# SyncE's transfers chained in the order of the plan, in an attention and feed-forward kernel of 394 tiles

## The chip, the cores and the metric

The kernel runs on one core of one Trainium2 chip. A core has five engines that each work through their own list of instructions in order: TensorE (PE in the profile, its weight loads PEld), VectorE (DVE), ScalarE (ACT), GpSimd (POOL) and SyncE (SP). In this kernel SP does no arithmetic: it issues all the transfers between DRAM and the core's memory, and within it, one after the other, and where a transfer must wait for something, SP waits with it. The transfers themselves are done by 16 DMA engines. The metric is the device time of one execution in microseconds (us), as the median of several runs.

## The reference, cut to what matters

Four batches of 12608 tokens with 128 channels attend to the keys through 49 agents, and the result goes through a feed-forward block of width 1024 with SoLU and a normalization.

```python
a2k = softmax(scale * agents @ k.T);  agent_v = a2k @ v      # per batch
q2a = softmax(scale * q @ agents.T);  x = q2a @ agent_v      # 50432 tokens in all
h = x @ w_in                                                 # 128 -> 1024
solu = h * softmax(h)
ln = (solu - mean(solu)) / sqrt(var(solu) + 1e-6) * g_ln
out = ln @ w_out                                             # 1024 -> 128
```

## The kernel before

The tokens of all four batches are laid end to end and cut into 394 tiles of 128, so that a tile can lie across two batches. Three kinds of work run interleaved.

*Per batch* (`phase_a`): the keys come in 13 blocks (tile kt, `kload`, L647), the values likewise (vt, `vload`, L658). PE multiplies the agents with a block of keys (L669), DVE and ACT make the running softmax, PE multiplies with the values (L723). In the end one matrix per batch is left, split in a high and a low part (mh, ml), which already holds w_in. The buffer kt is single (from the second batch on): a block can be loaded only when PE is through with the block before it. The same holds for vt.

*Per eight tiles* (`phase_b`): a load of queries (qt, `qload`, L891, also one buffer), PE's logits against the agents (L911), their softmax, and a transposed copy pT.

*Per tile*: PE makes ph = pT x (mh, ml) (L1027), DVE its maximum (nm, L1032), ACT the exponential (L1042), DVE the product u (L1047), ACT the square sum (L1053). Then 1024 x 128 of u must be transposed and multiplied with w_out, and units of four tiles alternate between two ways. A Y unit is transposed in blocks by DVE (tb, L1067) and moved into place by 16 transfers (uY, L1077), and PE multiplies it in one pass (L1083); its output oy (L1091 or L1093) is scaled by yp. A Z unit is transposed by PE (L1060), copied by ACT (uT), split by POOL (uH, uL) and multiplied by PE in three passes (L1154); DVE scales the product in place of a tile rB (L1238).

The scale factors yp and rB come by a detour: POOL computes them for two units, DVE turns them (yr, L1195), one transfer stores them in DRAM (dr, `send`, L1199), and two more read them back in the shapes that are wanted (yp, `senty`, L1225; rB, `sent`, L1204, spread over all partitions). L1238 frees a PSUM bank that PE needs for its next products, and the result goes out from the same tile (L1244).

What sets the order: every piece of work is an `op` of a planner (`Plan`) with its engine, an estimated cost, and a rank from a table. `plan.run` plays all engines through in modelled time, picks at each step the ready piece with the lowest rank, and writes its instructions down at that moment. This gives one list for all engines in the order of the plan. Afterwards the framework's own scheduler goes over the list and orders the instructions of each engine anew by its own estimates, unless a dependency holds them. The last lines of the kernel put such dependencies in, each instruction on the one before it on its engine, without a semaphore ("NoSync"), but for the engines in `engs` only:

```python
for ins in list(nc.cur_bb.bb.instructions)[marks:]:
    if ins.engine not in engs:
        continue
    if ins.engine in prev:
        tc.add_manual_dep(ins, prev[ins.engine], nosync, reason="order")
    prev[ins.engine] = ins.name
```

Before, `engs` (L451) holds PE, ACT, DVE and POOL; SP's transfers are left to the framework's scheduler.

Of the kernel before, what the change touches and what calls it, by code (L numbers as in the profile page):

```python
# [335 lines left out]
def kernel(  # L336
# [111 lines left out]
    DFX = 8.0  # L448
    ASTART = 4.99
    AEND = -155.17  # L450
    engs = (mybir.EngineType.PE, mybir.EngineType.Activation, mybir.EngineType.DVE, mybir.EngineType.Pool)  # L451
    SCALE = 1.0 / math.sqrt(C)
    INV = 1.0 / DF
    LIFT = DF ** 1.5
# [1098 lines left out]
```

## Time and profile before

| | us |
|---|---|
| median of 3 runs | 1466.27 (1463.65 to 1466.43) |
| profiled execution, its own time | 1469.04 |
| span in the profile, first to last instruction | 1467.3 |
| busy: PE, DVE | 1429.0, 1369.8 |
| busy: ACT, POOL | 1273.6, 978.4 |
| mean granted clock of PE, share of full speed | 0.992 |

Busy time is the union of an engine's instructions. Issuing transfers is not counted as busy, so SP has no row; its issues show in the timeline as SPq. A row of a timeline gives start, duration, engine, line, operation, tiles, and in brackets the idle time before and what ended it. Where rows are merged, x tells how many instructions they hold.

### The profile page before, as it was taken

To read this page: it belongs to the slowest core of one execution; us is meant where nothing else is said; L and a number is where in the kernel's file an instruction comes from. 1 tells how busy PE (TensorE), PEld (TensorE's weight loads), DVE (VectorE), ACT (ScalarE), POOL (GpSimd) and SP (SyncE) were. 2 spreads that over 40 slices of the span, in tenths; PEclk is the share of its full clock that TensorE was granted. 3 is DMA by queue.
4 is the path that set the end of the run, shared out by engine and by line. 5 is a ranking of instruction groups with operands and counts; after the bars stand their busy time and mean duration, and the time that the engine had idled before them with its cause. 6 is when DMAs were issued, how large, how long until landed. Compare 5 with 4: busy or idle time off the path is not lost.

```text
span 1467.3 us, 32448 instructions
## 1 busy us (share of the span) xinstructions
PE 1429.0 (97%) x11965; PEld 1268.3 (86%) x11965; DVE 1369.8 (93%) x1979; ACT 1273.6 (87%) x2424; POOL 978.4 (67%) x1125
## 2 busy tenths in 40 slices
PE   8799999999999999999999999989999999999998
PEld 4678899898898889989998888878988899999888
DVE  7899999999999989999999999979997999999985
ACT  5599999989889879989989899978987899889985
POOL 3476668766766766775766767666675678677664
PEclk9899999999999999999999999999999999999999
DMA  9456664564555475556546755545644555455351
GB/s 365 149 158 181 176 192 131 142 158 109 148 160 175 136 200 137 169 166 173 147 105 163 182 165 154 159 131 138 156 110 122 141 141 138 124 131 133 92 125 63
DMA packets 111647, 221.71 MB, mean 151 GB/s; under 512 B 46208, under 2 KB 49152, under 8 KB 111488
## 3 DMA queue, kind: packets, MB, share of 16 engines
q1 hardware_dynamic: 111488, 219.63, 54.7%
q8 instruction: 95, 1.56, 0.5%
q14 instruction: 64, 0.52, 0.1%
HBM read 92.87 MB, written 26.02 MB: 81 GB/s over the span
## 4 chain that ended last, share of the span: by engine, by line
PE 65%; DVE 16%; DMA 7%; ACT 6%; issue 3%; SPq 3%; POOL 1%; DVEq 0%; ACTq 0%
PE ph L1027 18%; PE px L1083 16%; PE px L1154 13%; PE px L1060 8%; DVE u L1047 5%; DVE nm L1032 5%; DMA rB<-dr 3%; ACT e L1042 3%; PE px L723 3%; DVE tb L1067 3%; PE px L911 2%; SPq L1077 2%; PE px L669 2%; ACT e L1053 2%; PE px L956 1%
## 5 line engine op out<-in xcount | busy, mean ns | idle before, releaser
L1042 ACT ACTIVATE e<-ph,nm 128x1024 f32<-128x1024 f32 x394 | 441.2, 1123 | 82.4 <-DVE nm L1032 79.3
L1047 DVE SCALAR_TENSOR_TENSOR u<-ph,e 128x1024 f32<-128x1024 f32 x394 | 471.6, 1216 | 26.4 <-ACT e L1042 23.4
L1053 ACT ACTIVATE e<-u,su 128x1024 bf16<-128x1024 f32 x394 | 455.1, 1160 | 33.1 <-DVE u L1047 32.7
L1032 DVE TENSOR_REDUCE nm<-ph 128x1 f32<-128x1024 f32 x394 | 464.9, 1205 | 13.5 <-PE ph L1027 12.8
L1138 POOL TENSOR_TENSOR uL<-uT,uH 128x1024 fp32r<-128x1024 f32 (+1 forms) x197 | 468.4, 2379 | 11.7
L1134 POOL TENSOR_SCALAR uH<-uT 128x1024 fp32r<-128x1024 f32 (+1 forms) x197 | 206.6, 1049 | 278.9 <-ACT uT L1125 273.3
L1083 PE MATMUL px<-w,uY 128*128 128x128 f32 x3072 | 374.4, 276 | 0.1
L1083 PEld LDWEIGHTS px<-w,uY 128*128 128x128 f32 x3072 | 357.8, 192 | 5.4 <-issue 2.3
L1027 PE MATMUL ph<-mh,pT 128*128 128x512 f32 x784 | 332.8, 424 | 7.0 <-DVE u L1047 6.9
L1027 PE MATMUL ph<-ml,pT 128*128 128x512 f32 x784 | 311.0, 397 | 0.0
L1067 DVE STREAM_TRANSPOSE tb<-u 128x1024 f32<-128x1024 f32 x192 | 235.4, 1233 | 0.8
L1154 PE MATMUL px<-uH,wH 128*128 128x256 f32 x808 | 233.2, 289 | 2.4 <-DVE rB L1238 1.3
L1125 ACT COPY uT<-px 128x512 f32<-128x512 f32 x392 | 220.1, 591 | 15.3 <-PE px L1060 13.8
L1060 PE MATMUL px<-ident,u 128*128 128x128 f32 x1616 | 226.4, 275 | 6.9 <-DVE u L1047 2.9
L1154 PE MATMUL px<-uL,wH 128*128 128x256 f32 x808 | 225.2, 279 | 0.0
L1154 PE MATMUL px<-uH,wL 128*128 128x256 f32 x808 | 225.2, 279 | 0.0
L1060 PEld LDWEIGHTS px<-ident,u 128*128 128x128 f32 x1616 | 186.4, 141 | 34.1 <-DVE u L1047 3.2
L1027 PEld LDWEIGHTS ph<-mh,pT 128*128 128x128 f32 x784 | 149.0, 190 | 47.0 <-DVE u L1047 19.9
L1027 PEld LDWEIGHTS ph<-ml,pT 128*128 128x128 f32 x784 | 149.6, 191 | 21.6
L1154 PEld LDWEIGHTS px<-uH,wH 128*128 128x128 f32 x808 | 152.4, 189 | 6.9 <-issue 2.7
L1154 PEld LDWEIGHTS px<-uL,wH 128*128 128x128 f32 x808 | 152.9, 189 | 2.3 <-issue 0.5
L1154 PEld LDWEIGHTS px<-uH,wL 128*128 128x128 f32 x808 | 152.3, 188 | 0.0
(134 smaller groups left out, 1465.4 us busy)
## 6 DMA issues: line engine op xcount, KB each, us to landing
uY<-tb SPq DMA_DIRECT2D x768, 128.0 KB, 2.4
qt<-in_qT_dram SPq DMA_DIRECT2D x49, 512.0 KB, 4.6
kt<-in_kT_dram SPq DMA_DIRECT2D x36, 512.0 KB, 4.9
vt<-in_v_dram SPq DMA_DIRECT2D x36, 512.0 KB, 4.5
rB<-dr SPq DMA_DIRECT2D x50, 256.0 KB, 4.1
out_dram<-rB SPq DMA_DIRECT2D x50, 256.0 KB, 2.4
out_dram<-oy SPq DMA_DIRECT2D x48, 256.0 KB, 2.5
kh<-in_kT_dram SPq DMA_DIRECT2D x12, 512.0 KB, 10.2
```

What stands on the lines that cost most here:

```text
L1027: nc.tensor.matmul(phs[x][:, sl], lhs, mats["mh" if m == 0 else "ml"][:, sl], start=(m == 0 and h != 1), stop=(m == 1 and h != 0))
L1032: nc.vector.tensor_reduce(out=nms[x], in_=phs[x], op=ALU.max, axis=AX.X, negate=True)
L1042: nc.scalar.activation(out=es[x], in_=phs[x], func=AF.Exp, bias=nms.pop(x), accum_out=st[G]["S"][:, j : j + 1])
L1047: nc.vector.scalar_tensor_tensor(out=u, in0=phs[x], scalar=INV, in1=es[x], op0=ALU.mult, op1=ALU.mult, accum_out=su)
L1053: nc.scalar.activation(out=sq, in_=u, func=AF.Square, bias=su, scale=-float(DF), accum_out=st[G]["Q"][:, j : j + 1])
L1060: nc.tensor.transpose(pt[:, kf * P : (kf + 1) * P], us[x][0][:, k0 * P : (k0 + 1) * P], ident)
L1067: nc.vector.transpose(to, us[x][0].rearrange("p (k r c) -> p k r c", r=GT, c=SQB))
L1083: nc.tensor.matmul(st[G]["po"][:, a * P : (a + 1) * P], yb[G][1][:, a, kf].rearrange("p x c -> p (x c)"), w2[:, kf, :], start=(kf == 0), s ...
L1125: nc.scalar.copy(out=rr[x][:, hf * 4 : hf * 4 + 4, :], in_=pt)
L1134: nc.gpsimd.tensor_scalar(out=uH, in0=rr[x][:, k0:k1, :], scalar1=1.0, scalar2=0.0, op0=ALU.mult, op1=ALU.add)
L1138: nc.gpsimd.tensor_tensor(out=uL, in0=rr[x][:, k0:k1, :], in1=uH.bitcast(F32), op=ALU.subtract)
L1154: nc.tensor.matmul(po, wt[:, kf, :], ut[:, kf, :], start=(q == 0), stop=(q == WM - 1))
```

## The change

SP is added to the engines whose instructions are chained.

```diff
-    engs = (mybir.EngineType.PE, mybir.EngineType.Activation, mybir.EngineType.DVE, mybir.EngineType.Pool)
+    engs = (mybir.EngineType.PE, mybir.EngineType.Activation, mybir.EngineType.DVE, mybir.EngineType.Pool, mybir.EngineType.SP)
```

The lists of PE, DVE, ACT and POOL stay as they are. Of SP's 1182 transfers 15 change places against the others: the first loads of keys and values of three batches, one further block of keys, two loads of queries near them, two outputs of Y units, and two pairs of yp and rB. The first keys of the third batch go 113 places back, its first values 43; the first keys and values of the fourth 22 each; the two outputs 18 and 19; the others 2 or 3 places forward or back. In the rows below a name ends in a running number of the program.

SP in the last batch, the transfers around the eleventh block of its keys (kt_10), before:

```order
L1199 DMA dr_12059<-yr_12057 16x2x32
L647 DMA kt_10_12188<-in_kT_dram 128x1024
L1225 DMA yp_12106<-dr_12059 128x4x1
L1204 DMA rB_12110<-dr_12059 128x512
L1244 DMA out_dram<-rB_12110 128x512
L891 DMA qt_12199<-in_qT_dram 128x1024
```

The same place with the change:

```order
L1199 DMA dr_12059<-yr_12057 16x2x32
L1225 DMA yp_12106<-dr_12059 128x4x1
L1204 DMA rB_12110<-dr_12059 128x512
L1244 DMA out_dram<-rB_12110 128x512
L647 DMA kt_10_12188<-in_kT_dram 128x1024
L891 DMA qt_12199<-in_qT_dram 128x1024
```

The keys have moved from in front of yp and rB to behind the output of rB.

SP after the last batch's keys, at two pairs of yp and rB some 30 us apart (a piece of the difference, - before, + with the change):

```order
 L1199 DMA dr_13823<-yr_13821 16x2x32
-L1077 DMA uY_13883<-tb_13506 32x1024 x2
 L1225 DMA yp_13844<-dr_13823 128x4x1
 L1204 DMA rB_13848<-dr_13823 128x512
-L1077 DMA uY_13883<-tb_13506 32x1024 x14
+L1077 DMA uY_13883<-tb_13506 32x1024 x16
 L1244 DMA out_dram<-rB_13848 128x512
```

Two pieces of uY that stood ahead of yp and rB now stand behind them; at the second pair it reads the same.

SP at the start of the third batch, where its first keys and values (kt_0, vt_0) now stand, with the change:

```order
L891 DMA qt_5026<-in_qT_dram 128x1024
L1244 DMA out_dram<-rB_4898 128x512
L647 DMA kt_0_5115<-in_kT_dram 128x1024
L658 DMA vt_0_5121<-in_v_dram 128x1024
L891 DMA qt_5170<-in_qT_dram 128x1024
L1244 DMA out_dram<-oy_5165 128x512
L1077 DMA uY_5177<-tb_4966 32x1024 x9
```

Before, kt_0 stood more than a hundred transfers earlier, and the queries qt_5170 behind the first two pieces of uY.

## Rows read from the trace of the kernel before

**Rows 1.** The page, part 1: busy us, share of the span, instructions of each engine.
```profile
PE 1429.0 (97%) x11965; PEld 1268.3 (86%) x11965; DVE 1369.8 (93%) x1979; ACT 1273.6 (87%) x2424; POOL 978.4 (67%) x1125
```

**Rows 2.** Waits, whole span: who waited, for whom; us in total, times, longest.
```profile
DVE rB L1238 <- DMA rB<-dr: 21.9, 16, 5.9
```

**Rows 3.** Timeline of SP, 956 to 1004.
```profile
970.69 0.56 SPq L1199 DMA_DIRECT2D dr<-yr  x1
979.28 0.33 SPq L647 DMA_DIRECT2D kt<-in_kT_dram  x1
...
980.14 0.49 SPq L1204 DMA_DIRECT2D rB<-dr  x1
```

**Rows 4.** Tile dr, 960 to 990: from issue to landing of dr, yp, rB.
```profile
DMA to landing us min/median/max: 1.7/3.4/3.7
```

**Rows 5.** Chain that ended last, 972 to 1062: start, us, what.
```profile
978.24 1.03 PE px L669 x4
...
984.63 1.95 PE px L911 x32
```

**Rows 6.** Timeline of DVE, 966 to 1000.
```profile
975.67 2.32 DVE L1032 TENSOR_REDUCE nm<-ph 128x1 f32<-128x1024 f32 x2
983.88 0.69 DVE L1238 TENSOR_TENSOR rB<-px,rB 128x512 f32<-128x512 f32 x1 [5.89 <-DMA rB<-dr]
...
990.35 2.49 DVE L1032 TENSOR_REDUCE nm<-ph 128x1 f32<-128x1024 f32 x2 [1.50 <-PE ph L1027]
```

**Rows 7.** Windows: us, busy of PE PEld DVE ACT POOL; PEclk, DMA, GB/s.
```profile
984.50:991.00 6.50, 6.37 (x55) 5.48 (x56) 5.00 (x11) 3.77 (x8) 0.00 (x0) 0.51 0.56 171
...
1137.00:1150.00 13.00, 12.40 (x93) 11.01 (x92) 12.45 (x17) 11.43 (x22) 8.34 (x9) 1.00 0.64 169
```

**Rows 8.** Line L1204 (rB), whole span: from issue to landing.
```profile
DMA to landing us min/median/max: 3.0/4.1/6.0
```

**Rows 9.** Timeline of SP, 1114 to 1136.
```profile
1123.12 0.56 SPq L1199 DMA_DIRECT2D dr<-yr  x1
1129.63 1.16 SPq L1077 DMA_DIRECT2D uY<-tb  x2
...
1131.46 0.56 SPq L1204 DMA_DIRECT2D rB<-dr  x1
```

**Rows 10.** Timelines of DVE and PE, 1122 to 1142, and of DVE, 1160 to 1172.
```profile
1135.44 0.69 DVE L1238 TENSOR_TENSOR rB<-px,rB 128x512 f32<-128x512 f32 x1 [2.95 <-DMA rB<-dr]
...
1136.66 1.09 PE L1060 MATMUL px<-ident,u 128*128 128x128 f32 x8 [1.77 <-DVE logits L923]
...
1165.05 0.69 DVE L1238 TENSOR_TENSOR rB<-px,rB 128x512 f32<-128x512 f32 x1 [0.88 <-DMA rB<-dr]
```

**Rows 11.** Waits of SP, 262 to 312.
```profile
SPq L647 <- PE px L669: 11.7, 1, 11.7
...
SPq L1199 <- DVE yr L1195: 3.9, 1, 3.9
```

**Rows 12.** Timelines of SP and PE, 59 to 82 and 407 to 426.
```profile
59.89 9.44 SPq L891 DMA_DIRECT2D qt<-in_qT_dram  x2
...
77.48 1.08 PE L669 MATMUL px<-kt,ag_sb 128*64 128x512 f32 x4
...
415.32 0.34 SPq L1244 DMA_DIRECT2D out_dram<-rB  x1
...
422.10 1.04 PE L669 MATMUL px<-kt,ag_sb 128*64 128x512 f32 x4
```

**Rows 13.** Keys, from issue to landing: tile kt, then the first batch's tile kh.
```profile
DMA to landing us min/median/max: 2.4/4.8/8.6
...
DMA to landing us min/median/max: 5.4/10.2/11.2
```

**Rows 14.** Line L1077 (uY), 425.4 to 427: from issue to landing.
```profile
DMA to landing us min/median/max: 4.3/4.4/4.4
```

**Rows 15.** The page, part 6: issues of uY, KB each, median us to landing.
```profile
uY<-tb SPq DMA_DIRECT2D x768, 128.0 KB, 2.4
```

## The prediction

> **What bounds the kernel now.** I read four views, in this order. The page first: PE is busy 97% of the span and DVE 93% [rows 1], so no engine has room, and an edit that only reorders SyncE's transfers (SP below) can win no more than the waits in which PE or DVE stand for a transfer. Next the list of waits: the reader should look for a compute engine on the left and DMA on the right. After the first tens of microseconds one line carries nearly all of them: DVE's product of rB (L1238, the last step of a Z unit) waits 21.9 us for the transfer that brings rB back from DRAM, in 16 places, 5.9 us in the longest [rows 2]. Then the timeline of SP at the places where the diff moves an rB, and last the timelines and the chain there, for who is held by it.
>
> **Place A, span 970 to 991.** SP issues dr at 970.69, and it lands 1.7 us later (the smallest of the three landings in its row), at 972.4. From there yp and rB could go. They don't: the next transfer in SP's order is a block of keys, kt_10, whose buffer is free only when PE's product of kt_9 (L669) has ended, at 978.24 + 1.03 = 979.27. So kt_10 leaves at 979.28 and rB only at 980.14 [rows 3 to 5]. DVE has finished its work at 975.67 + 2.32 = 977.99, waits 5.89 us at rB and starts it at 983.88. PE's next product (L911) needs the PSUM bank that this step frees, and goes from 979.27 to 984.63: 5.36 us idle [rows 5, 6]. After that idle time the granted clock is 0.51 over 6.5 us, the lower level of 1.2 and 2.4 GHz [rows 7].
>
> With the change kt_10 stands behind rB and its output. yp leaves at 972.4, rB about half a microsecond later (kt_10, yp and rB were issued within 0.86 us of one another [rows 3]), at 972.9. With the median landing of 4.1 us [rows 8] it is there at 977.0, before DVE asks at 977.99. DVE's 5.89 us go whole, the step ends 0.69 us later at 978.7, before PE has done L669, so PE's 5.36 us go too. PE without idle time keeps the upper clock, on which the 6.5 us of work take 6.5 x 0.51 = 3.3: another 3.2 us, 8.5 for PE. DVE gains 5.9 and the 1.50 us in which it stood for PE's slow products at 990.35 [rows 6]: 7.4. The later of the two sets what follows: **7.4 us**. Ends: with rB's slowest landing, 6.0 us [rows 8], it arrives at 978.9, DVE still waits 0.9, and if no clock comes back the gain is 5.0; if PE alone decides, 8.5. What is late next is nothing on SP: kt_10, delayed behind the output of rB (DVE free at 978.7), leaves within a microsecond of where it left before, when nobody waited for it.
>
> **Place B, 1123 to 1150.** dr leaves at 1123.12; two uY pieces in front of yp and rB are held until 1129.63, because PE still reads the uY buffer; rB leaves at 1131.46 and DVE waits 2.95 us for it [rows 9, 10]. With the change yp and rB go first: with dr as at A and the slowest rB that is 1123.12 + 1.7 + 0.5 + 6.0 = 1131.3, and DVE was free at 1135.44 - 2.95 = 1132.49. The uY pieces lose nothing, being held anyway. DVE gains 2.95. PE had stood 1.77 us for DVE's next step [rows 10] and, until 1150, another 13.00 - 12.40 = 0.60 us [rows 7], which I give back too: **2.4 us**, ends 1.8 (PE's first wait alone) and 3.0 (DVE's).
>
> **Place C, 1155 to 1170.** The same swap in the next unit but one; DVE waited 0.88 us there [rows 10]. **0.9 us**, ends 0 and 0.9.
>
> **What is moved and costed at nothing.** The third batch's first keys, kt_0, stood 113 transfers earlier and held SP for 11.7 us. That looks like a prize and is none: dr, the small transfer two places behind, afterwards still waited 3.9 us for DVE [rows 11]; SP was early. In their new place kt_0 and vt_0 follow an output issued at 415.32 for 0.34 us, so the keys leave at about 415.75. PE asks at 422.10 [rows 12], 6.35 us later; keys land in 4.8 us in the median [rows 13]: covered, by 1.5 us. With the slowest landing of 8.6 they would be 2.25 us late, the end on this side. In the second batch kt_0 follows two loads of queries that end at 59.89 + 9.44 = 69.33; PE asks at 77.48, 8.1 us on: covered by 3.3, and 0.5 us late at worst [rows 12, 13]. The first keys and values of the fourth batch move back by 22 transfers only. Two outputs (oy) go behind a group of uY: nobody on the chip reads an output, and its buffer is wanted two Y units later; the uY pieces win one issue, about 0.4 us, with no one waiting for them.
>
> **Sum.** 7.4 + 2.4 + 0.9 = **10.7 us**. The profiled execution took 1469.04 us (span 1467.3), so it would take 1458.3. Its own time is 2.8 us above the median of the runs shown, 1466.27; against that median I forecast **1455.6 us**.
>
> **A rule against it.** The pieces of uY issued right behind a load of queries near 425 land after 4.3 to 4.4 us, where 2.4 is the median of all 768 [rows 14, 15]. The Trainium skill, "DMA: Bandwidth & Descriptors", section "Queues, rings and completion order", says why that may be: a DMA engine's completion write lands only after all its earlier writes, so a small transfer behind a big one reports late; by that rule each bulk load that the change puts ahead of small ones costs those their delay. The trace agrees at this place. In the rows the delay is 2.0 us.
>
> **Rivals.**
> *Small transfers behind bulk.* The change puts loads of 512 KB in front of uY groups at two starts of a batch (near 424 and 768). If a reader stood waiting, each place would cost the 2.0 us above: 10.7 - 4.0 = 6.7, 1459.6 us. For it stands the delay itself [rows 14]. Against: no such wait of PE or DVE for uY shows in the list there. 6%.
> *Nothing moves.* The three gains are given back: what comes 7 to 8 us earlier then waits for something else, or the transfers are not issued in the order that is written. 1466.3 us. Against: in place A PE, DVE and ACT all stand still, so that all of them move together, and the order rows show SP's transfers moved. 9%.
> *Keys come late, and the kernel is slower.* Both first blocks of keys now go out late, with 8.1 and 6.35 us to spare where they had tens. If both need L us to land, PE, whose order is fixed, stands L - 8.1 and L - 6.35, and at each loses the 3.2 us of lower clock seen at place A: 2L - 14.45 + 6.4. That eats 10.7 at L = 9.4, and makes the kernel measurably slower from L = 10.8. The loads of the first microseconds did take 10.2, 11.2 at most [rows 13]: at 11.2 the cost is 14.35, the time 1466.3 + 3.65 = 1469.9 us. Against: those shared the engines with a dozen others, and the keys of later stretches took 4.8. 5%.
>
> **How the numbers follow.** A measurement of this kernel tells about 0.2%, 2.9 us, from no change. The forecast has 80%: gains from 5.0 + 1.8 + 0 = 6.8 to 8.5 + 3.0 + 0.9 = 12.4, 1459.5 to 1453.9 us. With 2.25 us for late keys above, and below the 2.6 us by which the fastest run lies under the median, the range is 1451.5 to 1462. Faster: 0.80 + 0.06 = 0.86; same 0.09; slower 0.05.
>
> **What would show it.** Right: in the list of waits DVE's line for rB falls from 21.9 us to about 12, its longest from 5.9 to under 3; SP issues rB within a microsecond of dr's landing at all three places; PE's wait of 5.4 us at L911 and the stretch at half clock behind it are gone. Place A is wrong if rB is issued early and DVE still waits there, or if the clock falls all the same. The forecast is wrong if PE waits at L669 for keys near 77 or 422, or if DVE's waits for rB move to other units.

## The result, and the profile with the change

| | before | with the change |
|---|---|---|
| median, first measurement | 1466.27 (5 runs: those shown above and two more) | 1452.75 (1450.73 to 1454.97, 5 runs) |
| ratio, 95% interval | | 0.991 (0.9896 to 0.9925) |
| median, measured again later | 1464.53 (1462.03 to 1469.37, 11 runs) | 1452.3 (1452.04 to 1454.52, 6 runs) |
| ratio, 95% interval | | 0.9914 (0.9897 to 0.9931) |
| profiled execution: time, span | 1469.04, 1467.3 | 1454.97, 1453.2 |
| mean granted clock of PE | 0.992 | 0.996 |

The kernel is faster by 13.5 us in the first measurement and by 12.2 in the second; 10.7 were forecast, and 1455.6 us. The answers to [rows 1, 2] first, the page's part 1 and the list of waits (us in total, times, longest) with the change:

```profile
PE 1424.3 (98%) x11965; PEld 1263.9 (87%) x11965; DVE 1370.4 (94%) x1979; ACT 1273.0 (88%) x2424; POOL 978.8 (67%) x1125
...
DVE rB L1238 <- DMA rB<-dr: 13.4, 12, 2.7
```

DVE's busy time is what it was, PE's is 4.7 us less: the same products, fewer of them at the lower clock. DVE's waits for rB have lost 8.5 us, from 21.9 to 13.4, and the longest has gone from 5.9 to 2.7 (about 12 and under 3 were forecast). Place A, the timelines of SP and of DVE with the change (start, us, engine, line, tiles; the answers to [rows 3, 6]):

```profile
972.04 0.56 SPq L1199 DMA_DIRECT2D dr<-yr  x1
973.78 0.38 SPq L1225 DMA_DIRECT2D yp<-dr  x1
974.21 0.50 SPq L1204 DMA_DIRECT2D rB<-dr  x1
979.96 0.34 SPq L1244 DMA_DIRECT2D out_dram<-rB  x1
980.64 0.33 SPq L647 DMA_DIRECT2D kt<-in_kT_dram  x1
...
977.02 2.32 DVE L1032 TENSOR_REDUCE nm<-ph 128x1 f32<-128x1024 f32 x2
979.26 0.67 DVE L1238 TENSOR_TENSOR rB<-px,rB 128x512 f32<-128x512 f32 x1
```

rB is issued 2.17 us after dr, where it was 9.45 before, and DVE goes from nm straight to rB: no bracket, no idle time. The keys leave 1.12 us after PE has begun L669, as long as before (1.12 in the same view), and no one waits for them. PE, and the clock around it (the windows view: us, busy of PE, PEld, DVE, ACT and POOL, then PEclk, DMA, GB/s; the answers to [rows 5, 7]):

```profile
979.52 1.08 PE L669 MATMUL px<-kt,ag_sb 128*64 128x512 f32 x4
980.43 1.09 PE L911 MATMUL px<-ag_sb,qt 128*64 128x49 f32 x32
...
970.00:992.00 22.00, 22.00 (x202) 20.04 (x202) 22.00 (x33) 20.28 (x40) 13.17 (x17) 1.00 0.47 131
```

PE and DVE are both busy for all of these 22 us, at the full clock. Places B and C in the timelines of SP and DVE (the answers to [rows 9, 10]):

```profile
1116.23 0.56 SPq L1199 DMA_DIRECT2D dr<-yr  x1
1117.97 0.38 SPq L1225 DMA_DIRECT2D yp<-dr  x1
1118.40 0.50 SPq L1204 DMA_DIRECT2D rB<-dr  x1
1122.74 7.49 SPq L1077 DMA_DIRECT2D uY<-tb  x12
...
1125.51 0.68 DVE L1238 TENSOR_TENSOR rB<-px,rB 128x512 f32<-128x512 f32 x1
...
1154.19 0.65 DVE L1238 TENSOR_TENSOR rB<-px,rB 128x512 f32<-128x512 f32 x1
```

Both waits of DVE are gone. Last the keys that go out late with the change, the timelines of SP and PE at the starts of the third and second batches (the answers to [rows 12]):

```profile
416.77 0.34 SPq L1244 DMA_DIRECT2D out_dram<-rB  x1
417.16 0.42 SPq L647 DMA_DIRECT2D kt<-in_kT_dram  x1
...
423.54 1.04 PE L669 MATMUL px<-kt,ag_sb 128*64 128x512 f32 x4
...
75.76 1.08 PE L669 MATMUL px<-kt,ag_sb 128*64 128x512 f32 x4
```

PE begins 6.38 us after the issue at the one place, and without idle time at both.

**Where the time went.** PE runs the same 11965 products in the same order in all the traces, so the start of each can be set against its start before. The table gives by how much that lead of a kernel over the profiled execution of before grows in each stretch (times of before; minus is lost). The kernels of the last five columns are those of the experiments.

| stretch | change | again | A alone | B and C | others alone | three places | before, chained |
|---|---|---|---|---|---|---|---|
| 0 to 55 | 1.9 | 1.9 | 1.1 | 2.0 | 1.6 | 1.7 | 0.2 |
| 55 to 965 | -3.2 | -0.4 | 0.5 | -0.8 | -2.3 | -0.2 | 0.8 |
| 965 to 1130 (A) | 8.2 | 8.2 | 8.2 | 0.2 | 1.4 | 8.1 | 1.1 |
| 1130 to 1153 (B) | 3.0 | 3.1 | -0.4 | 3.1 | 0.0 | 3.1 | 0.0 |
| 1153 to 1172 (C) | 1.0 | 0.9 | 0.3 | 0.9 | 0.0 | 0.9 | 0.0 |
| 1172 to the end | 3.2 | 3.2 | 2.1 | 3.4 | 4.1 | 3.1 | 0.8 |

The rows of A, B and C give 12.2 us together. The first and the last row I don't put down to the change: the kernel with the other moves alone has 5.7 us there as well and, timed, is no faster than before. In the last stretch SP's order is moreover the same in all these kernels: no transfer behind 1172 was moved in any of them. The profiled execution of before was one of the slower of its kind (1469.04, against medians of 1463.8 to 1464.9 in four later sets of 11 to 20 runs), and these rows show where.

The row of A is no firmer than the execution that it is measured against. The three columns that leave place A as it was ought to have nothing there, and they have 0.2 (B and C), 1.1 (before, chained) and 1.4 (others alone). Against them A is worth 6.8 to 8.2 us.

### The profile page after: what moved, and what is told of

It is laid out like the page before. It is cut to its first block, busy times and chain, and to the rows that moved or that the text cites. A ratio compares the mean times of both kernels' runs of the same rounds, so it can differ in the third digit from the quotient of the medians.

```text
span 1453.2 us, 32441 instructions
## 1 busy us (share of the span) xinstructions
PE 1424.3 (98%) x11965; PEld 1263.9 (87%) x11965; DVE 1370.4 (94%) x1979; ACT 1273.0 (88%) x2424; POOL 978.8 (67%) x1125
## 4 chain that ended last, share of the span: by engine, by line
PE 62%; DVE 17%; DMA 7%; ACT 6%; SPq 4%; issue 3%; POOL 1%; DVEq 0%; ACTq 0%; POOLq 0%
PE ph L1027 17%; PE px L1083 15%; PE px L1154 12%; PE px L1060 8%; DVE u L1047 5%; DVE nm L1032 5%; DMA rB<-dr 3%; ACT e L1042 3%; DVE tb L1067 3%; SPq L1077 3%; PE px L723 2%; PE px L669 2%; PE px L911 2%; ACT e L1053 2%; PE px L956 1%
## 5 line engine op out<-in xcount | busy, mean ns | idle before, releaser
L1138 POOL TENSOR_TENSOR uL<-uT,uH 128x1024 fp32r<-128x1024 f32 (+1 forms) x197 | 468.4, 2378 | 11.7
L1060 PE MATMUL px<-ident,u 128*128 128x128 f32 x1616 | 225.8, 274 | 3.8 <-DVE u L1047 2.8
L1060 PEld LDWEIGHTS px<-ident,u 128*128 128x128 f32 x1616 | 186.5, 141 | 30.5 <-DVE u L1047 3.9
```

What stands on the lines that cost most here:

```text
L1060: nc.tensor.transpose(pt[:, kf * P : (kf + 1) * P], us[x][0][:, k0 * P : (k0 + 1) * P], ident)
L1138: nc.gpsimd.tensor_tensor(out=uL, in0=rr[x][:, k0:k1, :], in1=uH.bitcast(F32), op=ALU.subtract)
```

## The experiments

All use the changed kernel and put SP's transfers in an order of their own before they are chained; other engines keep theirs. The edit against the changed kernel, here with the list of the run with the late keys:

```diff
-    prev = {}
...
+    lists = {}
     for ins in list(nc.cur_bb.bb.instructions)[marks:]:
-        if ins.engine not in engs:
-            continue
-        if ins.engine in prev:
-            tc.add_manual_dep(ins, prev[ins.engine], nosync, reason="order")
-        prev[ins.engine] = ins.name
+        if ins.engine in engs:
+            lists.setdefault(ins.engine, []).append(ins)
+    sp = lists[mybir.EngineType.SP]
+    rank = {i: float(i) for i in range(1, len(sp) + 1)}
+    MOVES = [(328, 330.5)]
+    for a, to in MOVES:
+        rank[a] = to
+    at_rank = {x.name: rank[i] for i, x in enumerate(sp, 1)}
+    sp.sort(key=lambda x: at_rank[x.name])
+    for chained in lists.values():
+        for a, b in zip(chained, chained[1:]):
+            tc.add_manual_dep(b, a.name, nosync, reason="order")
```

Only the list MOVES differs (transfer, new place). Below stands what that does to SP's order. The first four were timed in one set, beside a kernel before of 1463.85 us (1462.6 to 1466.88, 15 runs).

**Place A alone.** The order before, but:

```diff
-L647 DMA kt_10_12188<-in_kT_dram 128x1024
 L1225 DMA yp_12106<-dr_12059 128x4x1
 L1204 DMA rB_12110<-dr_12059 128x512
 L1244 DMA out_dram<-rB_12110 128x512
+L647 DMA kt_10_12188<-in_kT_dram 128x1024
```

> SP in the order of the kernel before, with one transfer moved: kt_10 of the last batch stands behind rB and its output (place A). My theory: DVE's 5.9 us at rB, PE's 5.4 us and the half clock behind them go, 7.4 us, so a ratio of about 0.995 and 1459 us; DVE's waits for rB fall from 21.9 to about 16 us. Rival (the gain comes from the order as a whole, or is given back behind the place): less than 4 us.

Measured: 1456.86 us (1456.66 to 1457.31), ratio 0.9951 (0.9938 to 0.9963): 7.0 us between the medians, 5.4 to 9.1 by the interval.

**Places B and C alone.** The order before, but at each of the two pairs:

```diff
-L1077 DMA uY_13883<-tb_13506 32x1024 x2
 L1225 DMA yp_13844<-dr_13823 128x4x1
 L1204 DMA rB_13848<-dr_13823 128x512
-L1077 DMA uY_13883<-tb_13506 32x1024 x14
+L1077 DMA uY_13883<-tb_13506 32x1024 x16
```

> SP in the order of the kernel before, with yp and rB ahead of the two uY pieces at places B and C only. My forecast gave 3.3 us for the two; the trace of the changed kernel shows about 4.2 there (3.2 and 1.0). Theory: 3 to 4.5 us, about 1462.5 us. Rival (PE, busy there, takes only its own wait of 1.8 us): 1.8 us, 1464.5 us.

Measured: 1457.9 us (1457.43 to 1461.02), ratio 0.9964 (0.9951 to 0.9976): 5.3 us by the ratio (3.5 to 7.2), 6.0 between the medians. The medians lie above the 3 to 4.5 expected, the interval takes in most of it; the prediction's 3.3 is just outside.

**The other moves alone.** The change, with the edits of A, B and C undone: `MOVES = [(799, 795.5), (914, 917.1), (915, 917.2), (936, 939.1), (937, 939.2)]`.

> SP in the order of the change, but with places A, B and C put back as they were before: what is left are the moved first keys and values, the queries near them and the two outputs. Theory: no change, within 2 us of the kernel before, 1466 us, and DVE's 5.9 us at rB is back. First rival (the moved loads win the extra 2 to 3 us that the change gained over the sum): 1463 to 1464 us. Second rival (keys come late): above 1469 us, with PE waiting for kt at L669 near 77 or 422.

Measured: 1464.42 us (1462.16 to 1467.93, 11 runs), ratio 1.0001 (0.9992 to 1.001). Nothing.

**The three places without the other moves.** The order before with both edits above.

> SP in the order of the kernel before with places A, B and C changed and nothing else. Theory: all of the gain, 1452 to 1455 us, as the whole change. Rival (the other moves carry 2 to 3 us of it): 1455.5 to 1457 us. If the other moves cost something (the trace of the changed kernel is some 2 us later than the one of before between 330 and 520), this one is faster than the change, 1450 to 1452 us.

Measured: 1452.42 us (1450.9 to 1455.81), ratio 0.9926 (0.9912 to 0.9939): 11.4 us between the medians, 8.9 to 12.9 by the interval. Places A, B and C hold the gain as far as these intervals tell; the rest of the change can be left out.

The next four stood beside a kernel before of 1463.84 us (1461.71 to 1467.48, 20 runs).

**The order before, chained.** All moves undone, so that SP's list is the one of before, word for word.

> The order of SP before the change, exactly, but fixed by the chain. Theory (the order is all that counts, the chain costs and gives nothing): the same time as before, within 0.2%, and all three waits at A, B and C are in its trace (5.9, 2.95 and 0.9 us of DVE). If the chain itself did something, the time would move without any transfer having changed its place. A second question: the trace of the kernel before has a stretch at lower clock at 42 to 49 us and an rB whose issue took 1.91 us at 1422.86; in the traces of the first four experiments both are weaker or gone. If they are scatter of one execution, this trace has not both of them in full; if they belong to the order before, it has.

Measured: 1464.57 us (1462.57 to 1468.24, 12 runs), ratio 1.0003 (0.9994 to 1.0013). The chain by itself does nothing. Waits, the timelines of DVE and PE at place A, and the clock behind it (windows view), in its trace:

```profile
DVE rB L1238 <- DMA rB<-dr: 25.0, 17, 5.9
...
982.91 0.69 DVE L1238 TENSOR_TENSOR rB<-px,rB 128x512 f32<-128x512 f32 x1 [5.87 <-DMA rB<-dr]
...
983.66 1.95 PE L911 MATMUL px<-ag_sb,qt 128*64 128x49 f32 x32 [5.34 <-DVE rB L1238]
...
983.50:990.00 6.50, 6.34 (x63) 5.62 (x64) 5.84 (x12) 3.90 (x9) 0.00 (x0) 0.70 0.52 159
```

The stall of place A is the same as in [rows 5, 6], to a few hundredths. But the clock in the 6.5 us behind it is 0.70 where it was 0.51 in [rows 7]: PE idled equally long and came back to the upper level some 2 us sooner. The fall itself had come earlier in PE's idle time. The windows view of PE's idle time, in the trace of before and in this one:

```profile
979.24:984.60 5.36, 0.00 (x1) 0.00 (x0) 0.72 (x2) 0.53 (x2) 1.46 (x1) 0.95 0.51 147
```

```profile
978.30:983.60 5.30, 0.02 (x2) 0.00 (x0) 0.69 (x2) 0.52 (x2) 1.43 (x1) 0.71 0.55 149
```

With a mean of 0.95 nearly all of the lower level fell on PE's products; with 0.71 more of it fell where PE had nothing to do. This is the 1.1 us of the table. The second question got the answer that speaks for the order: this trace has both, the lower clock at 40 to 50 (0.66 in both traces, 1.00 with the change) and the slow issue of rB, 1.83 us near 1421. Two things speak against it. The kernel with B made worse has the order before up to 1121, and gained 2.0 us in the first 55 all the same; A alone, B and C, and the three places, which keep the order before up to 965, gained 1.1 to 2.0. And if the 3 us at the end were the order's, place A alone would have gained 9 to 10 us, and the other moves alone 3; timed they gained 7.0 and nothing. So I leave both out of the change's gain; where they come from is open.

**Only B.** The edit of B in the order before, without that of C.

> The order before with place B alone: one yp and one rB in front of two pieces of uY. The prediction had 2.4 us for it (1.8 to 3.0) and 0.9 for C; the run with B and C gave more than the sum of them. If B is the term that was too small: 3 to 4 us here. If the surplus came from elsewhere: 2.4.

Measured: 1459.92 us (1458.14 to 1462.93), ratio 0.9971 (0.9961 to 0.9982): 3.9 us, 2.6 to 5.7 by the interval. The prediction's 2.4 lies outside. In its trace B is worth 3.05 us of PE's products.

**B made worse.** The order before, with yp and rB behind five more pieces:

```diff
-L1077 DMA uY_13883<-tb_13506 32x1024 x2
+L1077 DMA uY_13883<-tb_13506 32x1024 x7
 L1225 DMA yp_13844<-dr_13823 128x4x1
 L1204 DMA rB_13848<-dr_13823 128x512
-L1077 DMA uY_13883<-tb_13506 32x1024 x14
+L1077 DMA uY_13883<-tb_13506 32x1024 x9
```

> The order before with place B made worse: yp and rB behind seven pieces of uY instead of two, five issues of 0.63 us each or 3.2 us later. Theory (while nothing else is late, DVE's whole wait there is paid by all engines): DVE waits 6.1 us at this rB, and the time grows by 3.2, to about 1467.2. With a fall of the clock as at place A, where PE stood 5.4 us, 2 to 3 more: 1470. Rival (PE and ACT have work to go on with and catch up): under 1 us more, 1464 to 1465.

Measured, in a set with a kernel before of 1464.87 us (15 runs): 1468.26 us (1466.05 to 1471.52, 11 runs), ratio 1.002 (1.0008 to 1.0032): 3.4 us slower between the medians. Timelines of DVE and PE at B, and the clock behind it:

```profile
1137.15 0.69 DVE L1238 TENSOR_TENSOR rB<-px,rB 128x512 f32<-128x512 f32 x1 [6.50 <-DMA rB<-dr]
...
1138.37 1.97 PE L1060 MATMUL px<-ident,u 128*128 128x128 f32 x8 [5.32 <-DVE logits L923]
...
1139.00:1146.00 7.00, 7.00 (x47) 6.83 (x46) 6.85 (x10) 6.13 (x11) 4.12 (x4) 0.75 0.66 202
```

DVE's wait grew from 2.95 to 6.50, by 3.55, and PE's from 1.77 to 5.32, by the same. With 1.77 us of idle time the clock had stayed at the full rate in [rows 7]; with 5.32 it falls. In this trace PE's products fall back by 3.6 us at the wait and by another 1.9 at the lower clock; 1.3 of it is back by 1153, so that the stretch of B costs 4.2. Timed, 3.4 is seen, with 1.2 to 4.7 by the interval: the rival's "under 1 us" is out, and so is the wait with the whole price of the clock, 5 to 6 us. Together with the run before it, this shows B's price in both directions: in the traces, what rB is late is paid in full, in PE as in DVE, and of the lower clock on top only a part.

**The keys behind the queries.** The changed kernel, with the first keys of the third batch behind the next load of queries:

```diff
-L647 DMA kt_0_5115<-in_kT_dram 128x1024
 L658 DMA vt_0_5121<-in_v_dram 128x1024
 L891 DMA qt_5170<-in_qT_dram 128x1024
+L647 DMA kt_0_5115<-in_kT_dram 128x1024
 L1244 DMA out_dram<-oy_5165 128x512
```

> The changed kernel with one transfer moved: the first keys of the third batch go out behind the queries that follow them, about 7 us later (near 424.2 where they went at 417.16). PE asks for them at 423.54. Theory (a late transfer costs what PE waits, and the lower clock on top): with the landing of 4.7 us that they had, PE stands 5.4 us at L669 and then runs 3 us behind at the lower clock, as at place A: 1452.8 + 8.4 = about 1461; at least 5. Rival 1 (DVE and ACT work on meanwhile and PE, not alone the bound, catches up): 0 to 3 us. Rival 2 (the keys land later than 4.7, behind the values): over 10 us.

Measured: 1458.32 us (1457.03 to 1460.28), ratio to the kernel before 0.996 (0.9947 to 0.9973); against the 1452.3 us of the change 6.0 more, or 6.7 by the two ratios. Timelines of SP and PE, and the window behind it:

```profile
421.52 0.33 SPq L891 DMA_DIRECT2D qt<-in_qT_dram  x1
421.90 0.42 SPq L647 DMA_DIRECT2D kt<-in_kT_dram  x1
...
427.40 1.97 PE L669 MATMUL px<-kt,ag_sb 128*64 128x512 f32 x4 [5.92 <-DMA kt<-in_kT_dram]
...
429.00:436.00 7.00, 7.00 (x40) 6.32 (x39) 4.59 (x8) 2.92 (x5) 2.74 (x6) 0.70 0.36 87
```

The theory's 5.4 of waiting is 5.9, because the keys landed after 5.5 us behind the queries. Against both traces of the changed kernel PE's products stand 8.8 us further back behind the stall than ahead of it (8.4 were expected): the wait of 5.9 and another 2.9 at the lower clock. Timed, 6.0 to 6.7 of them are seen. By the end 1.8 us of it are back against the first trace of the change, and 0.6 more are lost against the second; two executions of one order differ by that much (2.8 us with the order before). So the price of keys that come late, on which the rival of a slower kernel was worked out, is real; but the change leaves them in time.

**rB sooner at nine more places.** In the list of waits with the change DVE still waits for rB 12 times. At nine places rB stands behind a last piece of uY, an output, the values or its yp. The kernel has it sooner at all nine, on top of the change; four of them:

```diff
+L1204 DMA rB_1524<-dr_1496 128x512
 L658 DMA vt_3_1522<-in_v_dram 128x1024
-L1204 DMA rB_1524<-dr_1496 128x512
...
+L1204 DMA rB_4322<-dr_4261 128x512
 L1225 DMA yp_4299<-dr_4261 128x4x1
-L1077 DMA uY_4207<-tb_3925 32x1024 x2
-L1204 DMA rB_4322<-dr_4261 128x512
...
+L1204 DMA rB_10351<-dr_10308 128x512
 L1225 DMA yp_10344<-dr_10308 128x4x1
-L1204 DMA rB_10351<-dr_10308 128x512
...
+L1204 DMA rB_17201<-dr_17167 128x512
 L1244 DMA out_dram<-oy_17131 128x512
-L1204 DMA rB_17201<-dr_17167 128x512
```

> The changed kernel with nine more rB issued sooner: each in front of one piece of uY, an output, or the yp of its dr (in one case four transfers sooner), as soon as dr is back. Theory (each wait of DVE for rB is on the path): DVE's waits there are shortened by what the issue comes sooner, 0.33 + 0.63 + 0.87 + 0.67 + 0.63 + 0.45 + 0.58 + 0.63 + 0.43 = 5.2 us: about 1447.6. Rival (waits under 1 us are taken up by the slack of the other engines, or the uY pieces behind are late instead): no change, 1452.8. Between them: 1450, about half.

Measured: 1448.23 us (1447.09 to 1450.9), ratio 0.9892 (0.9877 to 0.9908). Once more:

> The change with the nine rB issued sooner, once more: 1448.23 us the first time; the kernel without the other moves gave 1451.09 on another chip, where its trace has a block of values that landed 2.1 us later at 518. If that is scatter: 1448 to 1450 here, under the change by 3 to 4. If the first figure was luck: 1451.

Measured: 1448.72 us (1446.8 to 1449.75), ratio 0.9888 (0.9875 to 0.9902). The waits in the two traces:

```profile
DVE rB L1238 <- DMA rB<-dr: 5.9, 6, 2.7
```

```profile
DVE rB L1238 <- DMA rB<-dr: 7.4, 6, 2.7
```

It beats the changed kernel by 3.6 to 4.1 us between the medians, 3.2 to 3.8 by the ratios, 60 to 80% of the 5.2. The two were timed in different sets, and the intervals of the ratios overlap; but seven of its eight runs lie under all eleven of the change. So an rB that is issued less than a microsecond sooner counts here too.

**The same without the other moves, and the change again.**

> The order before with places A, B and C and the nine rB issued sooner, without the other moves of the change. If those are worth nothing and the gains add up: 11.4 + 4.5 = 16 us under before, about 1448, as the kernel with the nine rB on top of the change. If the earlier keys stood in the way somewhere: over 1450.

> The changed kernel once more, beside many runs of the kernel before. Its gain was 13.5 us against five runs of before with a median of 1466.27; the kernel with the three places alone gained 11.4 against fifteen runs with a median of 1463.85. If the surplus over the forecast of 10.7 was in the median of before: 1452 to 1453 here beside about 1463.9, a gain of 11 to 12. If the other moves are worth 2 us: a gain over 13.

Measured, beside a kernel before of 1464.53 us: the change 1452.3 us, as in the table at the top; the other 1451.09 us (1448.6 to 1451.61), ratio 0.9899 (0.9879 to 0.9918), which misses the 1448. In its trace a block of values took 7.9 us to land near 513 where it took 5.2 in the trace of the version above, and PE waited 1.9 us for it. Whether that belongs to the order or to the execution isn't settled: the intervals of the ratios overlap.

## Why the prediction was right, point by point

**Place A, 7.4: held.** Timed alone, 7.0, though the interval would let in PE's 8.5 as well. All its steps show in the rows above: yp and rB leave 1.7 and 2.2 us after dr (forecast 1.7 and 2.2), DVE doesn't wait, PE doesn't wait, the clock stays up, the keys leave as late as before and nobody misses them. Against the profiled execution of before it is 8.2. There "the later of the two sets what follows" took DVE's 7.4 over PE's 8.5, and the products came out nearer to PE's. The clock makes the difference: the same 5.3 us of idle time was followed by a stretch at 0.51 in one execution and 0.70 in another, over 6.5 us that is 3.2 us or 1.9. The forecast read its figures from the first alone; against the other traces A's worth goes down to 6.8. That 7.4 came out between the two is in part luck.

**Place B, 2.4: the step that was too small.** I took PE's two waits, 1.77 and 0.60, for the whole. PE's products came forward by 3.05, as much as DVE's 2.95 of waiting and a little more. PE's start moved by 1.94 where its wait was 1.77, and by 1.1 where 0.60 of idle time stood. At the first of these the rest is the overlap of one product with the next, which is lost at an idle gap and which the gap doesn't show: with the change L1060 starts 0.16 us before the product ahead of it ends. That the rest of the 1.1 is of the same kind is my reading. The end of 3.0 was the right reading: DVE, at 93% busy, carries its wait on whole. "Only B" and "B made worse" show it in their traces; timed, 3.9 (2.6 to 5.7) and 3.4 (1.2 to 4.7) agree with it.

**Place C, 0.9: held**, 0.9 to 1.0 in all traces that have the edit.

**The moves at nothing: held.** Timed alone they give a ratio of 1.0001. The first keys of the third and of the second batch left 6.4 and 8.2 us ahead of their use, as worked out, and the stand of SP for 11.7 us was no prize.

**The sum.** 7.4 + 2.4 + 0.9 had 10.7; the three places measured 11.4 alone and the change 12.2 when it was measured again. B's 0.6 and up to 0.8 of A's clock are the difference. The first measurement's 13.5 has another 1.4 to 2.4 us in it because the 1466.27 us of before, on which the forecast stood, is above the medians of all four later sets; the forecast of 1455.6 us is 2.9 off for both reasons. The 13.5 is also above the 12.4 at which the three places' ends add up; 1452.75 us is in the range only by the 2.6 us that were put below for the scatter of before. The 12.2 and the 11.4 lie within the ends.

**The rivals.** "Nothing moves" and "keys come late, and the kernel is slower" are out: the waits are gone, and PE doesn't stand at L669 for the first keys of a batch. For later blocks it stands there 0.8, 1.1 and 0.5 us near 104, 157 and 444; before, 0.5 and 0.4 near 105 and 157, and in the second trace of the change 0.8 near 104 alone. "Small transfers behind bulk" is out as a price, not as a fact. Pieces of uY behind one load of queries at 425 to 428 land in the changed kernel after 3.8 us in the median. With queries and keys in front, in the run with the late keys, they take 5.7. The views of tile uY, from 425 to 428 in the changed kernel and from 422.8 to 425.5 in that run:

```profile
DMA to landing us min/median/max: 3.6/3.8/4.0
```

```profile
DMA to landing us min/median/max: 5.5/5.7/5.8
```

Against 2.4 for all pieces [rows 15] that is 1.4 and 3.3 us. By the Trainium skill, "DMA: Bandwidth & Descriptors", section "Queues, rings and completion order", the write that reports a transfer lands only after every earlier write of its DMA engine, so that more bulk in front would make a small transfer report later; the trace agrees, here with 1.9 us for the second load. Whether it is this order or simply the bytes that were queued ahead, no run here tells. In the traces of before, of the change and of the run with the late keys only PE's weight loads wait for uY, 0.2 and 0.4 us near 1050, and nobody waits where loads stand ahead of it, so it cost nothing.

## What to carry to other kernels

Where one engine issues all transfers in order, look in its timeline for a short transfer that stands behind one still waiting for a buffer: the wait is paid by the reader of the short one, and the long one gained nothing here from standing first. Count the reader's whole wait. Where the matrix engine stood with it for 5.3 to 5.9 us here, a lower clock came on top (0.51 to 0.75 over the 6.5 to 7 us behind it); what that costs differs between executions. Set a trace of before against a second one of the same order before giving a stretch of the difference to the change: here a second trace of the same order was 2.8 us shorter than the first.

## What was not expected of the hardware

SP's issues mostly take 0.3 to 0.6 us, but 32 of the 1182 in the trace of before took over 1 us, and 37 with the change, about one in 40 to 46 us. They come with transfers of the queue for instructions, 95 of them in the span. In windows from half a microsecond ahead of such an issue to half a microsecond behind it, the DMA view shows a packet of that queue in 28 of the 32; in windows of the same length at 40 other issues, in 3. With the change it is 34 of 37, against 6 of 40. Not every such packet does it: in the trace of before 55 of the 95 begin in such a window of some issue, and for 27 of these the issue is an ordinary one. That the one makes the other is a guess from these counts and was not tried.

What it costs depends on which transfer is hit. Timelines of SP near the end, before and with the change, and the DMA queues (packets, MB, share) in the window 1422.8 to 1424.8 of before:

```profile
1422.86 1.91 SPq L1204 DMA_DIRECT2D rB<-dr  x1
1424.81 0.43 SPq L1225 DMA_DIRECT2D yp<-dr  x1
```

```profile
1412.18 0.53 SPq L1204 DMA_DIRECT2D rB<-dr  x1
1412.75 1.82 SPq L1225 DMA_DIRECT2D yp<-dr  x1
```

```profile
q8 instruction: 1, 0.02, 4.5%
```

Before, it is an rB that DVE waits for, and it lands 6.0 us after the start of its issue; with the change it is the yp behind it, and rB lands after 3.9. In the traces of the kernels that were run it falls on rB in three (before, the order before chained, B made worse) and on yp or neither in the others. The stretch behind it (1425 to 1440) differs by 2 to 4 us between these groups. But the kernel with the other moves alone has the better case in its trace and is no faster than before when timed, so it is not a gain of the order as far as these runs show. What decides which issue is hit stays open.
